# Attention feeding a routed mixture of experts: table stores behind the last mask, four early doubles, first weights in pieces, range count moved to the second unit

## The chip, the core and the metric

The kernel runs on one core of a Trainium2 chip, in 32-bit floats. The metric is the device time of one execution in microseconds (us), as the median of three runs.

The engines are called as in the profile: PE is the matrix engine (TensorE) with its weight loads PEld, DVE is VectorE, ACT is ScalarE, POOL is GpSimd, SP is the sync engine. Each engine works through its own instructions in order. SP starts nearly all plain transfers. POOL starts the indirect ones, which store rows at computed places.

## The reference

```python
def _attn_ref(q, k, v, s):                     # q, k, v: (8, 8, 576, 64)
    scores = scale * np.matmul(q, k.transpose(0, 1, 3, 2))
    causal = np.triu(np.ones((S, S), dtype=bool), k=1)
    cum = np.cumsum(np.maximum(s, 0.0), axis=-1)
    bias = -(cum[:, :, :, None] - cum[:, :, None, :])
    scores = np.where(causal, -1000000000.0, scores + np.minimum(bias, 0.0))
    ...
    return np.matmul(attn, v)                  # attn: softmax of scores

def _moe_ref(x, w_gate, w_local, w1, w2):      # x: (8, 576, 512), 8 experts, F = 1024
    logits = np.einsum('bsd,de->bse', x, w_gate)
    local_gate = 1.0 / (1.0 + np.exp(-np.einsum('bsd,de->bse', x, w_local).squeeze(-1)))
    ...
            fresh_e = int(np.argmax(logits[b, s]))
            if s == 0 or local_gate[b, s] < 0.5:
                e = fresh_e
            else:
                e = prev_e if prev_e >= 0 else fresh_e
            ...
            h = np.maximum(x[b, s] @ w1[e], 0.0)
            out[b, s] = p[e] * (h @ w2[e])     # p: softmax of the logits
```

Each of the 8 x 576 rows that the attention yields goes to one of eight experts: its own best one or, where its local gate is at least one half, that of the row before it. So the rows of one expert are known only once all the rows are counted.

## The kernel before

**Attention.** Each of 8 batches has 4 pairs of heads, 32 pairs in all, and `attention` works in 33 slots. Slot n computes the scores of pair n (`scores`, units u = 0 to 3; matmuls L772 and L781 on PE, exponentials L774 and L782 on ACT) and the values of pair n-1 (`values`, L805 and L808, in two blocks `po0` and `po6`, which DVE scales into `xb` and `lb` at L811, L813 and L815). The exponentials carry no bias of their own: the cumulated `s` goes into the keys and the value rows (`weigh`, L751). The causal triangle is cut by `masked` (L757) on POOL: six `affine_select` in a slot, four for the tiles `e` and, last, two for the small tile `et` of the ragged end. The values of a pair need all of its masked tiles, a slot later. A batch's values (`vTb`, `va`, `vl`) are loaded by SP at the start of slots 4, 8, 12 and so on; the router's logits of a batch are sums over heads of value rows times the gate's weights `wbd` (`value_logits`, L732 and L737).

**Router.** It works in four groups of two batches, 18 columns of 128 rows each. `plan(slot, place, f)` hangs a step into one of four places of a slot: 0 after the first two score units, 1 after `po0`, 2 after the other score units, 3 at the slot's end. After a group's last slot n come `sums`, `product`, `codes`, two turns, `ranks` (three matmuls `pos`, L255 to L257), `rows` (the index `idx` of each row) and `gates`. Then `scatter` stores the group's rows with their index and gate, column by column, into `table` in DRAM, sorted by expert. Each store is a `put` (L294): POOL zeroes one element `gap` and issues one indirect transfer:

```python
self.nc.gpsimd.memset(self.gap, 0.0)
put = self.nc.gpsimd.indirect_dma_start(out=self.halves, in_=src, ...)
self.tc.declare_no_dep(put, group="puts", reason="no two rows of the table are the same")
```

Stores of different columns do not wait for one another. A read of the table waits for the stores before it, and a store waits for the reads before it, since which rows a read takes is known only at run time. The stores of a group were placed four a slot, two at place 1 and two at place 3, from slot n+3 on. `range_ends` (slot 5, one matmul `wep`, L721) gathers cumulated ends for the range count below.

**Experts.** `Experts.run` (L527) takes 24 units in the order of `ORDER`: D is 256 rows of one expert ("double"), S is 128 rows, M is two halves of 64 rows of two experts. `assign` chooses experts and rows of the units from the counts so far. Two doubles are chosen early (`EARLY`), from the counts of the first two groups, in slot 20, so that their weights (`load(0)`, 4 MB in two transfers, slot 23) and rows (`fetch(0)`, `fetch(1)`, slot 24) are on the way while attention still runs. There are four places for weights, and `load` puts one expert's `w1b` and `w2b` into the next one. `fetch(u)` on SP reads the rows of a unit (`xq`, four transfers a piece, L454) and its indices and gates (`gi`, L457) from the table; `turn_x` transposes them on DVE. `layer1` (L469; matmuls L481 for M, L490 for the others), a ReLU on ACT, `layer2` (L505; matmuls L516), the gate's product `y` on DVE (L519) and an indirect store into `out_dram` on POOL (L521) finish a unit. Behind the first layer of unit 0, whose chunks also hold the last group's router steps, stand 8 pads and the 18 stores of the last group, and the choice of all other units. From then on unit u's first layer is followed by `fetch(u + 2)`.

**Range count.** `in_range` (L901) counts on DVE which row sums and ends lie in a safe range (L910 to L917), sums the counts over partitions with a matmul against a tile of ones (`g_ones`, memset on POOL, L919; `g_total`, L921) and writes `out_of`. The program ends by reading that number on the engines; if it is not zero, a general version runs instead. It stood behind everything else.

## Time and profile before

| what | us |
|---|---|
| median of three runs (894.46, 892.03, 897.78) | 894.46 |
| the profiled execution | 900.83 |
| its span on the core | 898.9 |
| PE busy, share of the span | 808.7, 90% |
| POOL busy, share of the span | 214.9, 24% |
| ACT busy, share of the span | 162.0, 18% |
| DVE busy, share of the span | 246.0, 27% |
| matmuls of the experts' first layer, D and S (L490) | 226.1 |
| matmuls of the experts' second layer (L516) | 268.2 |
| issuing 72 table stores on POOL (L297) | 72.2 |

The span runs from the first to the last record of the core; the execution's own time has some 2 us more around it. Busy time is the sum over an engine's instructions. The table says that PE has by far the most work, and that about a tenth of the span it has none. It does not say where. The 72 stores keep POOL for 72.2 us in all, and POOL is idle for three quarters of the span, so as an average POOL is no limit. Whether it is one in the stretch where the stores stand is read from that stretch alone.

### The profile page before, as it was taken

The numbers are of one execution on the slowest core, as the hardware profiler recorded it, in microseconds if no ns is written. First come the engines' busy times: TensorE is split into PE (matmuls) and PEld (weight loads), VectorE is DVE, ScalarE is ACT, GpSimd is POOL, SyncE is SP. The second block draws the span as 40 slices with busy tenths as digits, with TensorE's granted clock in tenths as the row PEclk, the third lists the DMA queues.
The fourth block names the chain that finished last, engine by engine and source line by source line (L and its number), as shares of the span: only waits on it lengthen the run. The fifth ranks groups of instructions, "written<-read, shape, count | busy, mean of one in ns | idle before, by whom it ended". The sixth has DMA issues, their size and how long they took to land.

```text
span 898.9 us, 16140 instructions
## 1 busy us (share of the span) xinstructions
PE 808.7 (90%) x6578; PEld 532.7 (59%) x6578; DVE 246.0 (27%) x663; ACT 162.0 (18%) x292; POOL 214.9 (24%) x488
## 2 busy tenths in 40 slices
PE   6989878987878799549999999999999999999994
PEld 3767656766656576414663763676467556656663
DVE  3524714452344246004004104000400040022001
ACT  2334322322322220100110110110011100111010
POOL 1543257235624635701000000000000000000000
PEclk7999989988978999859999999999999999999998
DMA  8676264544682433979994993976896789587000
GB/s 233 184 215 185 81 188 140 171 133 146 250 254 69 149 131 116 348 283 282 376 290 155 413 272 146 426 245 229 294 399 235 206 335 354 199 247 315 24 22 18
DMA packets 60979, 196.72 MB, mean 219 GB/s; under 512 B 17053, under 2 KB 37021, under 8 KB 52192
## 3 DMA queue, kind: packets, MB, share of 16 engines
q1 hardware_dynamic: 52928, 175.48, 57.0%
q0 software_dynamic: 6880, 20.10, 6.0%
q8 instruction: 54, 0.88, 0.4%
q14 instruction: 29, 0.24, 0.1%
q10 hardware_dynamic: 1088, 0.02, 0.1%
HBM read 174.95 MB, written 21.14 MB: 218 GB/s over the span
## 4 chain that ended last, share of the span: by engine, by line
PE 60%; issue 3%; POOL 1%; DVE 0%; POOLq 0%
PE yp L516 30%; PE hp L490 25%; PE hp L481 5%; POOL table L297 1%; PE po L805 0%; POOL e L758 0%; DVE y L519 0%; DVE g_good L915 0%; DVE g_good L913 0%; DVE g_good L914 0%; DVE g_count L917 0%; PE po L808 0%; POOL et L758 0%; POOL gap L296 0%; DVE g_scaled L910 0%
## 5 line engine op out<-in xcount | busy, mean ns | idle before, releaser
L516 PE MATMUL yp<-w2b,hT 128*128 128x512 f32 (+1 forms) x704 | 268.2, 594 | 0.0
L490 PE MATMUL hp<-xT,w1b 128*128 128x256 f32 (+1 forms) x1152 | 226.1, 357 | 0.0
L490 PEld LDWEIGHTS hp<-xT,w1b 128*128 128x128 f32 x1152 | 198.9, 191 | 32.6 <-issue 10.3
L516 PEld LDWEIGHTS yp<-w2b,hT 128*128 128x128 f32 (+1 forms) x704 | 110.5, 175 | 150.1 <-issue 147.0
L521 POOL DMA_INDIRECT out_dram<-y,gi x38 | 37.2, 980 | 471.1 <-DVE y L519 449.3
L805 PE MATMUL po<-vg,e 128*64 128x75 f32 x3072 | 125.5, 240 | 24.6 <-POOL e L758 23.3
L805 PEld LDWEIGHTS po<-vg,e 128*64 128x64 f32 x3072 | 113.7, 144 | 32.1 <-POOL e L758 25.4
L774 ACT ACTIVATE e<-ps 128x1024 f32<-128x1024 f32 x96 | 95.3, 1023 | 197.4 <-PE ps L772 172.2
L492 ACT ACTIVATE hT<-hp 128x256 f32<-128x256 f32 (+1 forms) x144 | 51.9, 361 | 437.3 <-PE hp L490 437.3
L519 DVE TENSOR_SCALAR y<-yp,gi 128x512 f32<-128x512 f32 x38 | 28.3, 744 | 314.4 <-PE yp L516 314.4
L772 PE MATMUL ps<-qb,kb 64*128 64x512 f32 (+4 forms) x640 | 112.3, 481 | 0.2 <-DMA qb<-in_q_dram 0.2
L758 POOL TENSOR_SCALAR_AFFINE_SELECT e<-e 128x256 f32<-128x256 f32 x128 | 63.8, 521 | 109.5 <-ACT e L774 108.5
L772 PEld LDWEIGHTS ps<-qb,kb 64*128 64x128 f32 x640 | 61.9, 202 | 42.0 <-issue 32.7
L297 POOL DMA_INDIRECT table<-xb,idx x72 | 72.2, 1003 | 44.9 <-issue 19.4
L501 DVE STREAM_TRANSPOSE hT<-hs 32x256 f32<-32x256 f32 x96 | 41.8, 436 | 92.6 <-ACT hs L483 91.3
L481 PE MATMUL hp<-w1b,xT 128*64 128x512 f32 x192 | 45.5, 629 | 23.3 <-issue 23.3
L811 DVE RECIPROCAL recs<-po 128x12 f32<-128x12 f32 x64 | 13.6, 213 | 174.6 <-PE po L805 88.7
L481 PEld LDWEIGHTS hp<-w1b,xT 128*64 128x64 f32 x192 | 14.2, 144 | 50.7 <-issue 50.4
L466 DVE STREAM_TRANSPOSE xT<-xq 128x1024 f32<-128x1024 f32 (+1 forms) x24 | 24.4, 1015 | 35.7 <-DMA xq<-table 35.5
L751 DVE TENSOR_TENSOR vg<-va,wk 128x1184 f32<-128x1184 f32 (+1 forms) x16 | 31.8, 2031 | 0.0
L813 DVE TENSOR_TENSOR xb<-po,recs 128x384 f32<-128x384 f32 x64 | 29.3, 458 | 2.6 <-DVE recs L811 0.5
L758 POOL TENSOR_SCALAR_AFFINE_SELECT et<-et 64x64 f32<-64x64 f32 x64 | 15.4, 240 | 42.5 <-DMA table<-xb,idx 26.9
(212 smaller groups left out, 230.4 us busy)
## 6 DMA issues: line engine op xcount, KB each, us to landing
w1b<-in_w_dram SPq DMA_DIRECT2D x30, 2048.0 KB, 9.7
w2b<-in_w_dram SPq DMA_DIRECT2D x30, 2048.0 KB, 12.4
vTb<-in_vT_dram SPq DMA_DIRECT2D x8, 1280.0 KB, 8.8
kb<-in_k_dram SPq DMA_DIRECT2D x32, 288.0 KB, 3.2
qb<-in_q_dram SPq DMA_DIRECT2D x32, 288.0 KB, 3.8
va<-in_vm_dram SPq DMA_DIRECT2D x8, 1024.0 KB, 10.9
xq<-table SPq DMA_DIRECT2D x56, 130.0 KB, 7.5
xq<-table SPq DMA_DIRECT2D x48, 32.5 KB, 6.4
```

The source lines that it names most:

```text
L297: put = self.nc.gpsimd.indirect_dma_start(out=self.halves, in_=src, element_offset=0, in_offset=None, out_offset=bass.IndirectOffsetOnAxis ...
L481: mm(ps[d, :], lhsT=xT[:, k, d], rhs=self.ws[ls[i]][0][:, k, c * 512 : c * 512 + 512], start=(k == 0), stop=(k == DK - 1))
L490: mm(ps[:, :w], lhsT=self.ws[ls[0]][0][:, k, c * P : c * P + P], rhs=xT[:, k, :w], start=(k == 0), stop=(k == DK - 1))
L492: nc.scalar.activation(self.hT[u][:, c, :w], ps[:, :w], Act.Relu)
L501: self.nc.vector.transpose(hT[32 * a : 32 * a + 32, :, 32 * r : 32 * r + 32], hs[32 * r : 32 * r + 32].rearrange("p (c i) -> p c i", i=P)[ ...
L516: mm(ps[d, :], lhsT=hT[:, k, n * P + i * w : n * P + i * w + w], rhs=self.ws[ls[i]][1][:, k, :], start=(k == 0), stop=(k == FK - 1))
L521: put = nc.gpsimd.indirect_dma_start(out=self.out[:, :], out_offset=bass.IndirectOffsetOnAxis(ap=gi.bitcast(I32)[:, n, 0:1], axis=0), in_= ...
L751: nc.vector.tensor_tensor(vgs[b % 2][g].rearrange("p c h e -> p (c h) e")[:, :, : VW - 1], va.rearrange("p c h e -> p (c h) e")[:, : n * H ...
L758: nc.gpsimd.affine_select(out=ap, in_=ap, compare_op=Alu.is_ge, fill=0.0, base=0, pattern=n, channel_multiplier=-1)
L772: mm(ps[:, h, at : at + z - a], lhsT=kb[d, c * P : c * P + P], rhs=qb[d, a:z], start=True, stop=True)
L774: nc.scalar.activation(e, ps, Act.Exp, scale=scale)
L805: mm(po[d, j - j0, :], lhsT=weights_of(n, c, j, h), rhs=vg[:, c, 2 * hp + h, :], start=(c == 0), stop=(c == last))
```

## The change

What it does, part by part:

- **Stores.** A group's stores stand two a slot instead of four, both at place 3, behind the slot's last mask, from slot n+4 on. The first group has slots 12 to 20, the second 20 to 28, the third 28 to 32 and then eight stores at the start of `Experts.run` (`self.rest`). Slots 20 and 28 have four. `ranks`, `rows` and `gates` move to places 0, 1 and 3 of slot n+3. `idx` has two buffers, since a group's stores now outlast the next group's start.
- **`xb` by batch.** The tile of a group's rows becomes two tiles, one a batch, in four half-size buffers.
- **Four early doubles.** `EARLY` is `(2, 2)`: two chosen in slot 20, two more in slot 28 from the counts of three groups. `ORDER` becomes four D, then four times MDD, then twice MDSS: the same units in another order.
- **First weights in pieces.** `load(0)` goes in four pieces in slots 21 to 24. `fetch(0)` and `fetch(1)` move from slot 24 to slot 29, `turn_x(0)` from slot 28 to 31.
- **Start of the experts.** `run` issues the eight remaining stores, `load(1)`, `fetch(2)`, `turn_x(1)`, `fetch(3)`. Later the first layer of unit u is followed by `turn_x(u + 1)` and `fetch(u + 3)`.
- **Range count.** `in_range` stands behind the first layer of unit 1; its matmul uses a bank of the pool `ps_m`.
- **Small moves.** Router constants in slot 3; the matmul of the range ends in slot 6, a slot behind the work that feeds it; `wbd` is prepared outside the program and loaded in one transfer on SP, instead of a memset on POOL and four transfers on ACT.

The diff, cut to its core:

```diff
-EARLY = 2
+EARLY = (2, 2)
-ORDER = "DD" + "MDD" * 2 + "MDDS" * 4
+ORDER = "DDDD" + "MDD" * 4 + "MDSS" * 2
...
-        idx = st["idx"] = self.s("idx", [P, NC], I32)
+        idx = st["idx"] = self.s("idx", [P, NC], I32, bufs=2)
...
     def scatter(self, g, c):
         st = self.g[g]
-        self.put(st["x"][:, c].rearrange("p g f -> p (g f)"), st["idx"][:, c : c + 1])
+        self.put(st["x"][c // NJ][:, c % NJ].rearrange("p g f -> p (g f)"), st["idx"][:, c : c + 1])
...
-    def assign_early(self):
+    def assign_early(self, i):
+        v = self.nc.vector
         self.counted()
-        self.early, used, _ = self.assign("a", self.shifted("n0", 8), None, EARLY, DOUBLE)
...
+        of, used, _ = self.assign(f"a{i}", n, self.start, EARLY[i], DOUBLE)
+        self.early.append(of)
+        v.tensor_tensor(self.used, self.used, used, op=Alu.add)
...
-        self.p_x = self.x_stack.enter_context(tc.tile_pool(name="p_x", bufs=2, side="right"))
+        self.p_x = self.x_stack.enter_context(tc.tile_pool(name="p_x", bufs=2 * GB, side="right"))
+        self.rest = []
...
-    def load(self, l):
+    def load(self, l, part=None):
...
+        parts = 1 if part is None else 4
+        for t, src in zip(self.ws[l], (self.w1, self.w2)):
+            n = t.shape[1] // parts
+            c = slice((part or 0) * n, (part or 0) * n + n)
+            nc.sync.dma_start(t[:, c].rearrange("p c f -> p (c f)"),
+                              src[bass.ds(self.e, 1), :, c].rearrange("o p c f -> (o p) (c f)"))
...
+        for f in self.rest:
+            f()
         self.load(1)
+        self.fetch(2)
         self.turn_x(1)
+        self.fetch(3)
...
-                    self.fetch(2)
                 else:
-                    self.fetch(u + 2)
-                self.turn_x(u + 1 if u else 99)
+                    self.turn_x(u + 1)
+                    self.fetch(u + 3)
+                if u == 1:
+                    in_range(tc, recs, wend, router.over, out_of, self.ps_m)
...
-        in_range(tc, recs, wend, router.over, out_of)
...
-    nc.gpsimd.memset(wbd, 0.0)
-    for h in range(2):
-        for w, a, z in ((w_gate, 0, E), (w_local, E, E + 1)):
-            nc.scalar.dma_start(wbd[heads[h], :, h * WR + a : h * WR + z],
-                                w.rearrange("(a h d) e -> h d a e", h=2, d=DH)[h])
+    nc.sync.dma_start(wbd, wbd_in)
...
-        plan(n + 2, 2, lambda g=g: router.ranks(g, ps_m))
-        plan(n + 2, 3, lambda g=g: router.rows(g))
-        plan(n + 3, 1, lambda g=g: router.gates(g, of[g][0]))
+        plan(n + 3, 0, lambda g=g: router.ranks(g, ps_m))
+        plan(n + 3, 1, lambda g=g: router.rows(g))
+        plan(n + 3, 3, lambda g=g: router.gates(g, of[g][0]))
         for c in range(NC):
-            plan(n + 3 + c // 4, (1, 3)[c // 2 % 2], lambda g=g, c=c: router.scatter(g, c))
+            if n + 4 + c // 2 <= NPAIR:
+                plan(n + 4 + c // 2, 3, lambda g=g, c=c: router.scatter(g, c))
+            else:
+                experts.rest.append(lambda g=g, c=c: router.scatter(g, c))
+    plan(3, 3, router.constants)
+    plan(5, 1, range_ends)
+    plan(6, 0, range_ends_sum)
     n = 2 * HP * GB
-    plan(2, 3, router.constants)
-    plan(5, 3, range_ends)
-    plan(n + 4, 1, router.assign_early)
-    plan(n + 7, 3, lambda: experts.load(0))
-    plan(n + 8, 1, lambda: (experts.fetch(0), experts.fetch(1)))
-    plan(n + 12, 3, lambda: experts.turn_x(0))
+    plan(n + 4, 1, lambda: router.assign_early(0))
+    for i in range(4):
+        plan(n + 5 + i, 3, lambda i=i: experts.load(0, i))
+    plan(n + 13, 1, lambda: (experts.fetch(0), experts.fetch(1)))
+    plan(n + 12, 1, lambda: router.assign_early(1))
+    plan(n + 15, 3, lambda: experts.turn_x(0))
```

On POOL, one slot with stores, before. The names `e_...` are the tiles of exponentials, `et` that of the ragged end; `x2` is two instructions in a row:

```order
L758 AFFINE_SELECT e_2535<-e_2535 128x2x128
L758 AFFINE_SELECT e_2536<-e_2536 128x2x128
L296 MEMSET gap 1x1
L297 DMA table<-xb,idx 75264x260
L296 MEMSET gap 1x1
L297 DMA table<-xb,idx 75264x260
L758 AFFINE_SELECT e_2537<-e_2537 128x2x128 x2
L758 AFFINE_SELECT et<-et 64x64 x2
L296 MEMSET gap 1x1
L297 DMA table<-xb,idx 75264x260
L296 MEMSET gap 1x1
L297 DMA table<-xb,idx 75264x260
```

The first pair of stores stood ahead of the masks of the second half of the slot, and the second pair behind the last mask. On the same engine after the change, two slots in a row:

```order
L782 AFFINE_SELECT e_2121<-e_2121 128x2x128
L782 AFFINE_SELECT e_2122<-e_2122 128x2x128
L782 AFFINE_SELECT e_2123<-e_2123 128x2x128 x2
L782 AFFINE_SELECT et<-et 64x64 x2
L300 MEMSET gap 1x1
L301 DMA table<-xb,idx 75264x260
L300 MEMSET gap 1x1
L301 DMA table<-xb,idx 75264x260
L782 AFFINE_SELECT e_2286<-e_2286 128x2x128
L782 AFFINE_SELECT e_2287<-e_2287 128x2x128
L782 AFFINE_SELECT e_2288<-e_2288 128x2x128 x2
L782 AFFINE_SELECT et<-et 64x64 x2
```

Only two stores stand in a slot, behind its last mask; ahead of them there is nothing but masks. On SP, the end of attention after the change, from the last keys and queries to the weights of the second unit (TENSOR_LOAD reads the chosen expert and row from memory, ISA rows are address arithmetic):

```order
L651 DMA kb<-in_k_dram 128x576
L652 DMA qb<-in_q_dram 128x576
L437 TENSOR_LOAD a0of
L472 ISA
L472 DMA xq<-table 32x8x130
```

Both early fetches (four `xq` and one `gi` each) now stand behind the last keys and queries, with the second unit's weights behind them; before, they stood between the first unit's weights and the keys of later slots. On POOL, slot 29's two stores come after these reads of the table in the program, and the first of the two waits for all ten of them. On PE, the first units before; `xT` and `hT` are a unit's turned rows and hidden layer, `yp` its output:

```order
L490 MATMUL hp<-xT,w1b 128x256 x8
L516 MATMUL yp<-w2b,hT 128x512 x16
L490 MATMUL hp<-xT,w1b 128x256 x32
L481 MATMUL hp<-w1b,xT 64x512 x16
L516 MATMUL yp<-w2b,hT 128x512 x16
L516 MATMUL yp<-w2b,hT 64x512 x16
L490 MATMUL hp<-xT,w1b 128x256 x32
L516 MATMUL yp<-w2b,hT 128x512 x16
L490 MATMUL hp<-xT,w1b 128x256 x32
L481 MATMUL hp<-w1b,xT 64x512 x16
```

The second unit, a double, and the third, two halves (L481), were taken as a pair here: both first layers, then both second layers. After the change:

```order
L508 MATMUL hp<-xT,w1b 128x256 x8
L534 MATMUL yp<-w2b,hT 128x512 x16
L508 MATMUL hp<-xT,w1b 128x256 x32
L952 MATMUL g_total<-g_count,g_ones 128x1
L534 MATMUL yp<-w2b,hT 128x512 x16
L508 MATMUL hp<-xT,w1b 128x256 x32
L534 MATMUL yp<-w2b,hT 128x512 x16
L508 MATMUL hp<-xT,w1b 128x256 x32
L499 MATMUL hp<-w1b,xT 64x512 x16
L534 MATMUL yp<-w2b,hT 128x512 x16
```

Four doubles come first, and the range count's matmul (L952) stands between the first and the second layer of the second one. The tile of ones that it takes is set on POOL, where after the change these rows stand between the last pads and the outputs of the second unit:

```order
L301 DMA table<-pad,pad_i 75264x260
L300 MEMSET gap 1x1
L301 DMA table<-pad,pad_i 75264x260
L300 MEMSET gap 1x1
L301 DMA table<-pad,pad_i 75264x260
L538 MEMSET gap 1x1
L539 DMA out_dram<-y,gi 4608x512
L538 MEMSET gap 1x1
L539 DMA out_dram<-y,gi 4608x512
L950 MEMSET g_ones 128x128
L538 MEMSET gap 1x1
L539 DMA out_dram<-y,gi 4608x512
```

The memset of ones (L950) has moved from the end of the program to the place behind the first unit's two output stores; ahead of the pads shown stand the last group's 18 stores and the eight of the third group.

More of the change, by code (lines that the diff above doesn't have):

```diff
@@ L66 @@
     w_local: bass.AP,
+    wbd: bass.AP,
     w1: bass.AP,
@@ L85 @@
         with ExitStack() as early:
-            attention(early, tc, q, k, vm, vt, vT, s, w_gate, w_local, ident, recs, wend, router, experts)
+            attention(early, tc, q, k, vm, vt, vT, s, wbd, ident, recs, wend, router, experts)
         experts.run(recs, wend, out_of)
@@ L417, in piece @@
         if kind == "D":
-            of, n = (self.router.early, n) if n < EARLY else (self.router.doubles, n - EARLY)
+            if n < sum(EARLY):
+                of, n = self.router.early[n // EARLY[0]], n % EARLY[0]
+            else:
+                of, n = self.router.doubles, n - sum(EARLY)
         elif kind == "S":
@@ L818, in sums @@
     def sums(g):
-        xb, lb = xs.pop(g)
+        xb, lb = [xs.pop(b) for b in range(g * GB, g * GB + GB)], xs.pop((g, "l"))
         ls = p_ls.tile([P, NC, E + 1], F32, name="ls")
@@ L1437 @@
     v = i["v"]
+    wbd = _np.zeros((2, DH, HP, 2, WR), _np.float32)
+    for h in range(2):
+        for n, w in ((slice(0, E), i["moe_w_gate"]), (slice(E, E + 1), i["moe_w_local"])):
+            wbd[h, :, :, h, n] = w.reshape(HP, 2, DH, -1)[:, h].transpose(1, 0, 2)
     arrays = {
@@ L1446 @@
         "w_local": i["moe_w_local"],
+        "wbd": wbd.reshape(P, HP, 2 * WR),
         "w1": i["moe_w1"].reshape(E, DK, P, F).transpose(0, 2, 1, 3),
```

57 lines of the change are left out of this document (33 added, 24 removed).

## The prediction

> **What bounds the kernel now.** I read the busy time by stage first, then what TensorE (PE) waits for, then the queues behind those waits. The stages are cut at the first score matmul of slot 1, of slot 11, at the first expert matmul (328.46 us, called T below), at both ends of the expert stage's one gap and at the last matmul. Columns: stretch, its length, busy us and instructions of each engine, granted PE clock, DMA share, GB/s.
>
> ```profile
> 18.84:104.62 85.78, 78.39 (x1449) 60.43 (x1442) 40.56 (x114) 31.54 (x42) 33.10 (x99) 0.98 0.60 181
> 104.62:328.46 223.84, 183.92 (x2980) 140.84 (x2977) 86.60 (x269) 65.47 (x86) 111.19 (x239) 0.89 0.50 156
> 328.46:371.21 42.75, 42.73 (x168) 31.42 (x168) 22.75 (x104) 6.08 (x16) 21.26 (x41) 1.00 0.57 208
> 371.21:394.49 23.28, 0.00 (x0) 0.03 (x1) 0.71 (x1) 0.38 (x1) 8.06 (x16) 0.62 0.75 262
> 394.49:404.54 10.05, 10.05 (x33) 3.18 (x33) 0.00 (x0) 0.60 (x1) 0.00 (x0) 0.70 0.93 390
> 404.54:887.24 482.70, 482.68 (x1856) 289.94 (x1856) 87.35 (x152) 52.35 (x139) 36.80 (x70) 1.00 0.71 254
> 887.24:898.90 11.66, 0.35 (x2) 0.30 (x2) 3.57 (x9) 0.00 (x0) 1.20 (x2) 0.70 0.09 31
> ```
>
> PE is full in the experts except for one gap of 23.28 us. In slots 11 to 32, where the table is stored, it is idle for 223.84 - 183.92 = 39.9 us, and its clock stands at 0.89. The price of a slot without stores is that of slot 7, PE full at clock 1.00; the row below it is its value matmuls.
>
> ```profile
> 70.93:77.97 7.04, 7.04 (x128) 5.45 (x125) 5.89 (x9) 3.08 (x4) 3.99 (x5) 1.00 0.27 89
> L805 PE MATMUL po<-vg,e 128*64 128x75 f32 x96 | 3.6, 230 | 0.0
> ```
>
> PE's waits, first in slots 11 to 32, then in slots 1 to 10 (us in total, times, longest):
>
> ```profile
> PE po L805 <- POOL e L758: 22.0, 13, 2.7
> PE po L808 <- POOL et L758: 10.3, 4, 5.9
> PE pos L255 <- DVE incl L246: 5.3, 2, 2.6
> PE pos L255 <- DVE incl L246: 2.6, 1, 2.6
> PE wep L721 <- DVE ends L712: 2.0, 1, 2.0
> ```
>
> So masks on POOL hold PE, and ranks and range ends hold it where they follow their inputs at once. POOL's own rows say why its masks are late: four stores stand in a slot, and the last mask of a slot waits until the stores ahead of it have landed.
>
> ```profile
> 199.09 0.96 POOL L297 DMA_INDIRECT table<-xb,idx  x1 [0.21 <-issue]
> ...
> 206.65 0.24 POOL L758 TENSOR_SCALAR_AFFINE_SELECT et<-et 64x64 f32<-64x64 f32 x1 [5.63 <-DMA table<-xb,idx]
> 206.95 0.09 POOL L296 MEMSET gap<- 1x1 f32 x1
> 207.37 0.98 POOL L297 DMA_INDIRECT table<-xb,idx  x1 [0.33 <-POOL gap L296]
> 208.35 0.09 POOL L296 MEMSET gap<- 1x1 f32 x1
> 208.65 0.96 POOL L297 DMA_INDIRECT table<-xb,idx  x1 [0.21 <-issue]
> ...
> 239.36 0.96 POOL L297 DMA_INDIRECT table<-xb,idx  x1 [0.21 <-issue]
> ...
> 250.49 0.24 POOL L758 TENSOR_SCALAR_AFFINE_SELECT et<-et 64x64 f32<-64x64 f32 x1 [9.20 <-DMA table<-xb,idx]
> table<-xb,idx POOLq DMA_INDIRECT x72, 2.8
> ```
>
> A store with its memset takes 1.28 us (207.37 to 208.65). From its start it lands in 2.8 us (median), in 7.6 beside a batch's value loads (199.09 to 206.65), in 11.1 beside these and the first weights (239.36 to 250.49).
>
> **The change, part by part.** *Slots 11 to 32.* Clean, they would cost 21 x 7.04 = 147.8, a last slot of values alone 3.6 + about 0.3, value logits in four slots (1.5 each by the two rows below), three ranks at 0.7 (339.48 to 340.19 in the chain of waits) and two logit sums at an estimated 0.5: 161 us. They take 223.8, so 62.8 go to waits and to the slow clock that follows them.
>
> ```profile
> L732 PE MATMUL vwp<-vTb,wbd 128*32 128x128 f32 x128 | 4.3, 276 | 0.0
> L737 PE MATMUL vwt<-vTb,wbd 128*32 128x32 f32 x128 | 1.9, 197 | 0.0
> 339.48 0.12 PE pos L255 x2
> 339.60 0.35 PE pos L256 x2
> 339.95 0.24 PE pos L257 x2
> ```
>
> After the change a slot has two stores behind its last mask, and that mask waits for stores of the slot before. POOL's loop is the landing plus 2.0 us (206.65 to 208.65): with 2.8 it is 4.8, under the 7.04 of PE, and it stays under it up to a landing of 5.0. So I take the waits of PE on POOL as gone; what hides the stores is the 2.2 us that POOL then has free in each slot. Slots 20 and 28, with four stores, use that up for one slot. Ranks move a place behind their input, the store's first wait for the gates goes with them.
>
> What stays, or is new: (a) In the slots after value loads the landing of 7.6 exceeds 5.0 by 2.6, four times; half of it reaches PE, since the masks have some 3 us of slack: 4 us (0 to 10). (b) Four half-size buffers: batch 5's first write on DVE waits for batch 1's stores in slot 20; 2 us (0 to 4). (c) The row fetches of units 0 and 1 now stand in slot 29, between stores. They read the table, so slot 29's first store waits for all ten of them to land, and slot 30's masks are queued behind it.
>
> ```profile
> 259.71 1.92 SPq L454 DMA_DIRECT2D xq<-table  x4
> ...
> 265.81 0.40 SPq L457 DMA_DIRECT2D gi<-table  x1
> xq<-table SPq DMA_DIRECT2D x56, 130.0 KB, 7.5
> xq<-table SPq DMA_DIRECT2D x16, 65.0 KB, 20.5
> ```
>
> Counted from the start of slot 29: slot 28's four stores end at 5.4 and land at 7, issuing two fetches takes 6.5 (259.71 to 266.21), and the reads land 2 to 7.5 later (4 taken, little else is moving): 17.5. Without them the store would start at 7.4. Slot 30's first mask then ends at 20.5, where PE wants it at 16.1: 4.4 and a catch-up of 1.6 make 6 us (2 to 11).
>
> *Slots 1 to 10* lose the ranks (2.6 + 0.7) and the wait for the range ends (2.0): 85.78 becomes 80.5. The first weights of the gate come in one transfer on SP instead of four on ACT; PE then still waits for the next keys behind the same value loads, so I put that at 0 (-1 to +3). First expert matmul: 18.84 + 80.5 + 161 + 12 = 272.3, 56.2 earlier.
>
> *The gap.* Its old cause, unit 2 waiting for the last group's rows, goes: units 2 and 3 are early doubles. But the range count's matmul now stands behind unit 1's first layer, and it needs the ones, whose memset stands on POOL behind 8 remaining stores, the last group's 18, 8 pads and unit 0's two output stores.
>
> ```profile
> 357.38 13.83 PE hp L490 x64
> 371.21 23.28 issue
> 343.97 1.01 POOL L297 DMA_INDIRECT table<-xb,idx  x1 [17.59 <-DVE n_i L322]
> ...
> 379.80 0.99 POOL L521 DMA_INDIRECT out_dram<-y,gi  x1 [0.25 <-issue]
> ```
>
> Before, that run of 28 starts at T + 15.5 and ends at T + 52.3. Now its first store also waits for the fetches of units 2 and 3, which wait for the 8 remaining stores: twelve stores of 1.28 from T - 3 end at T + 12.4 and land at T + 15, the fetches issue until T + 21.5 and land 4 later: T + 25.5, 10 us later than before. So the ones are there at T + 62.6, PE is there at T + 42.75 (the third stage's length): a new gap of 19.9 us (9.8 if the fetches cost nothing, 36 if they land after 20.5), with the same slow 10 us at clock 0.70 behind it. Against 23.28 that is a gain of 3.4; the matmul itself costs 0.35. I take off 1 us for weights near the end, where a fetch three units ahead makes SP wait for output stores (0 to 6). The same matmuls run otherwise: units and sizes are unchanged. Net 2.0.
>
> *The end.* 3.6 us of range count leave the chain behind the last matmul. But the last output store is issued at 888.3 too, and SP still waits for it after everything else:
>
> ```profile
> SPq L1455 <- DMA out_dram<-y,gi: 1.5, 1, 1.5
> ```
>
> That transfer then decides the end, so I take 0 (0 to 2).
>
> Sum: 56.2 + 2.0 + 0 = 58.2 us. The profiled execution took 900.83 us (span 898.9), 0.7% over the median of 894.46: 842.6 on its scale, 836 for the median.
>
> The Trainium skill, page "DMA: Bandwidth & Descriptors", section "SWDGE vs HWDGE vs iDMA", says that a DMA engine serves software and hardware queues in turn; by that a store's delay depends on a load being in flight and not on its size, and cutting the first weights in pieces only repeats the delay. The trace half agrees: 7.6 us beside value loads, 11.1 with the weights added, so size does count. By the rule the time is that of rival three.
>
> **Rivals.** *One: the fetches delay nothing* (their landing falls into POOL's other waits). The new gap is 9.8, (c) is 2: 836 - 10 - 4 = 822 to 826. For it: reads that nothing disturbs can land fast. Against: the wait is in the program, and 6.5 us of issue alone remain.
>
> *Two: the fetches land late.* With 20.5 us, the median of 16 fetches behind weights, the gap is 36 and the time 852. For it: unit 1's second weights and unit 2's stand in the same queue. Against: the first are issued at T, the second behind the fetches.
>
> *Three: the pieces repeat the delay.* Each of the four slots with a piece in flight has the 11.1 us landing once seen: 4 x (11.1 - 5.0) = 24, time 860. Against: 1 MB a slot is a quarter of what stood ahead of those stores.
>
> *Four, the other side: the landing wait takes the place of the one removed.* Every one of 21 slots pays landing - 5.0. At 7.8 us in all of them the whole 58 are gone (894), at 8.6 it is 911. For it: 7.6 and 11.1 were seen. Against: the median of 72 is 2.8, and only four slots of 21 have value loads.
>
> **How the numbers follow.** Forecast 836 (829 to 845): 0.54. One: 0.15. Two: 0.12. Three: 0.08. Four: 0.04. The rest, 0.07, is spread outside. 820 to 858 takes in the forecast, one and two. One per cent, about 9 us, is what a measurement here can tell from no change: every case but four is faster by more. Faster 0.95, same 0.02, slower 0.03.
>
> **What would show it.** Right: slots 12 to 28 near 7.04 us, no mask waiting for a store of its own slot, a wait of some 10 us on POOL ahead of slot 29's first store, the first expert matmul near 272, a PE gap of about 20 us in front of the range count's matmul, released by the memset of ones, and an end that still waits for the last output store. Wrong: masks still releasing value matmuls in most slots, no gap ahead of that matmul, or a gap in front of a pair's first layer late in the experts.

## The result, and the profile after

| | median, us | range, us | ratio to before (95% interval) |
|---|---|---|---|
| before, 4 runs | 896.12 | 892.03 to 899.03 | |
| after, 4 runs | 854.95 | 847.43 to 859.67 | 0.9536 (0.9449 to 0.9623) |

The change makes the kernel about 41 us faster. The predicted time was 836, so the median lies 19 us above it, inside the range of 820 to 858. The profiled execution took 851.99 us, its span is 850.3.

The busy time by stage, cut as in the prediction: slots 1 to 10, slots 11 to 32, the first expert unit, the one gap, the slow stretch behind it, the rest, the end. Columns as there: stretch, length, busy us and instructions of PE, PEld, DVE, ACT and POOL, granted clock, DMA share, GB/s.

```profile
18.81:99.42 80.61, 78.16 (x1437) 60.49 (x1437) 35.52 (x107) 31.42 (x42) 30.38 (x98) 0.96 0.62 187
99.42:278.75 179.33, 167.09 (x2985) 128.27 (x2983) 91.31 (x299) 65.15 (x86) 99.06 (x221) 0.99 0.61 189
278.75:325.25 46.50, 38.60 (x130) 25.78 (x128) 23.95 (x107) 3.17 (x9) 27.20 (x54) 0.93 0.69 233
325.25:343.35 18.10, 0.00 (x0) 0.00 (x0) 2.38 (x6) 0.38 (x1) 13.67 (x26) 0.60 0.75 294
343.35:355.23 11.88, 11.88 (x43) 10.01 (x44) 0.00 (x0) 2.27 (x7) 0.25 (x2) 0.75 1.02 427
355.23:843.20 487.97, 487.96 (x1888) 291.33 (x1888) 87.13 (x154) 53.25 (x141) 36.82 (x70) 1.00 0.67 250
843.20:850.30 7.10, 0.00 (x0) 0.00 (x0) 0.75 (x1) 0.00 (x0) 0.98 (x1) 0.80 0.11 43
```

Of the two rows of attention, the first became 5.2 us shorter and the second 44.5: in slots 11 to 32 PE's idle time fell from 39.9 to 12.2 us, its clock rose from 0.89 to 0.99. The experts (T to the end: 571.6 us, 570.4 before) gained nothing. A gap of 18.1 us stands near where the prediction had put one of 19.9. That looks like a confirmation, but its waits are others than the forecast ones. First what PE waits for, over the whole span (us in total, times, longest), then the same for ACT:

```profile
PE hp L508 <- issue: 18.1, 1, 18.1
PE ps L796 <- DMA qb<-in_q_dram: 5.3, 1, 5.3
PE lp L189 <- issue: 5.0, 1, 5.0
PE po L831 <- POOL e L782: 4.5, 2, 2.7
...
PE po L834 <- POOL e L782: 0.2, 1, 0.2
```

```profile
ACT hT L510 <- remote: 58.5, 3, 36.2
```

Masks on POOL now hold PE for 4.5 + 0.2 = 4.7 us, where it was 32.3. The gap stands in front of a first-layer matmul (L508), not of `g_total`, and nothing that the profile shows releases it ("issue"). ACT, which should take those products, is idle for 36.2 us and is released by something that the profile can't name either ("remote"). The start of the experts in time, PE, then ACT, then POOL of the same kernel (start, duration, engine and line, operation, count, idle time and releaser):

```profile
278.75 3.90 PE L508 MATMUL hp<-xT,w1b 128*128 128x256 f32 x16
...
306.17 13.90 PE L534 MATMUL yp<-w2b,hT 128*128 128x512 f32 x32
319.91 5.34 PE L508 MATMUL hp<-xT,w1b 128*128 128x256 f32 x24
343.35 11.76 PE L508 MATMUL hp<-xT,w1b 128*128 128x256 f32 x40 [18.11 <-issue]
354.95 0.28 PE L952 MATMUL g_total<-g_count,g_ones 128*128 128x1 f32 x2
```

```profile
291.31 0.38 ACT L510 ACTIVATE hT<-hp 128x256 f32<-128x256 f32 x1 [19.80 <-remote]
...
342.92 0.38 ACT L510 ACTIVATE hT<-hp 128x256 f32<-128x256 f32 x1 [36.16 <-remote]
```

```profile
277.13 0.98 POOL L301 DMA_INDIRECT table<-xb,idx  x1 [0.28 <-POOL gap L300]
...
278.42 0.96 POOL L301 DMA_INDIRECT table<-xb,idx  x1 [0.21 <-issue]
...
291.07 0.96 POOL L301 DMA_INDIRECT table<-xb,idx  x1 [0.22 <-issue]
...
306.33 1.01 POOL L301 DMA_INDIRECT table<-xb,idx  x1 [13.95 <-DVE be L341]
...
338.08 0.96 POOL L301 DMA_INDIRECT table<-pad,pad_i  x1 [0.23 <-issue]
...
339.35 1.00 POOL L539 DMA_INDIRECT out_dram<-y,gi  x1 [0.22 <-issue]
...
343.26 0.25 POOL L950 MEMSET g_ones<- 128x128 f32 x1
```

How to read them together: PE has the first product of the second unit ready some two microseconds after 319.91, as its 24 matmuls (three products of eight) run at full pace. ACT applies the first ReLU only at 342.92, and PE stops when its product buffers are full. The same happens to the first unit: its first product is begun at T = 278.75 and its first ReLU comes at 291.31, 12.6 us later, where 2.0 to 2.3 is usual. Both delays lie beside a dense run of stores on POOL, one every 1.27 us: twelve from 277.13 to 292.0, and 28 from 306.33 (the last group's stores, the pads and the first unit's outputs). Both end within a microsecond of the run's end. The second also ends at the memset of ones, so this trace alone can't tell it from the predicted cause.

### The profile page after: what moved, and what is told of

Read it like the earlier page. It is cut to its first block, busy times and chain, and to the rows that moved or that the text cites. A ratio compares the mean times of both kernels' runs of the same rounds, so it can differ in the third digit from the quotient of the medians.

```text
span 850.3 us, 16187 instructions
## 1 busy us (share of the span) xinstructions
PE 794.2 (93%) x6578; PEld 522.3 (61%) x6578; DVE 249.8 (29%) x692; ACT 161.2 (19%) x292; POOL 211.5 (25%) x491
## 4 chain that ended last, share of the span: by engine, by line
PE 82%; DMA 4%; issue 4%; POOL 2%; SPq 2%; another core or an unknown queue 2%; DVE 1%; ACT 1%; POOLq 0%; ACTq 0%; DVEq 0%
PE yp L534 31%; PE hp L508 26%; PE po L831 9%; PE ps L796 8%; PE hp L499 5%; DMA table<-xb,idx 3%; SPq L661 1%; DMA vTb<-in_vT_dram 1%; POOL table L301 1%; ACT e L798 1%; PE po L834 1%; PE pt L805 1%; POOL e L782 1%; PE vwp L756 1%
## 5 line engine op out<-in xcount | busy, mean ns | idle before, releaser
L508 PE MATMUL hp<-xT,w1b 128*128 128x256 f32 (+1 forms) x1152 | 232.9, 363 | 19.1 <-issue 18.1
L508 PEld LDWEIGHTS hp<-xT,w1b 128*128 128x128 f32 x1152 | 202.8, 194 | 54.7 <-issue 28.9
L831 PE MATMUL po<-vg,e 128*64 128x75 f32 x3072 | 118.1, 231 | 6.7 <-POOL e L782 4.5
L831 PEld LDWEIGHTS po<-vg,e 128*64 128x64 f32 x3072 | 107.1, 137 | 13.4 <-POOL e L782 4.8
L796 PE MATMUL ps<-qb,kb 64*128 64x512 f32 (+4 forms) x640 | 105.7, 454 | 5.7 <-DMA qb<-in_q_dram 5.3
L796 PEld LDWEIGHTS ps<-qb,kb 64*128 64x128 f32 x640 | 58.1, 190 | 45.1 <-issue 36.0
L837 DVE RECIPROCAL recs<-po 128x12 f32<-128x12 f32 x64 | 13.5, 211 | 120.3 <-PE po L831 60.9
L499 PE MATMUL hp<-w1b,xT 128*64 128x512 f32 x192 | 42.5, 595 | 0.0
```

The costliest lines, as they stand in the source:

```text
L499: mm(ps[d, :], lhsT=xT[:, k, d], rhs=self.ws[ls[i]][0][:, k, c * 512 : c * 512 + 512], start=(k == 0), stop=(k == DK - 1))
L508: mm(ps[:, :w], lhsT=self.ws[ls[0]][0][:, k, c * P : c * P + P], rhs=xT[:, k, :w], start=(k == 0), stop=(k == DK - 1))
L796: mm(ps[:, h, at : at + z - a], lhsT=kb[d, c * P : c * P + P], rhs=qb[d, a:z], start=True, stop=True)
L831: mm(po[d, j - j0, :], lhsT=weights_of(n, c, j, h), rhs=vg[:, c, 2 * hp + h, :], start=(c == 0), stop=(c == last))
```

## The experiments

The theories. **Ones:** the gap is that of the prediction, the second unit waits for the memset of ones behind POOL's stores. **Run:** a dense run of stores itself holds up what PE hands to ACT and DVE, so two stalls stand there, whatever waits for the ones. The runs were made in four groups, each on a chip of its own with the kernel before beside them (medians 896.25, 895.18, 893.61 and 893.92 us there). In the table "first ReLU" is counted from T, and "unit 1" from the start of DVE's work on the first unit's second output product to the second unit's last ReLU, which takes 13.8 us where nothing holds it up. "Gap" is a PE wait in front of `g_total`. The medians are over all runs of a kernel, the other numbers from its one trace. The expectations call Ones theory A and Run theory C; B says that the second unit's results reach ACT late for a cause of their own, D that the row fetches ahead of the run make the stalls, E that the chip or session does.

| kernel | chip | median, us | T | first ReLU | unit 1 | gap |
|---|---|---|---|---|---|---|
| before | | 896.12 | 328.4 | 2.2 | 13.8 | |
| after | | 854.95 | 278.7 | 12.6 | 31.9 | |
| e1, changed kernel | A | 857.13 | 280.3 | 15.7 | 37.7 | |
| e2, ones ready | A | 860.97 | 287.7 | 10.1 | 31.1 | |
| e3, count at the end | A | 863.79 | 290.7 | 8.9 | 31.7 | |
| e4, four a slot | A | 867.39 | 301.4 | 2.3 | 39.1 | |
| e5, spaced | B | 863.12 | 284.8 | 2.0 | 13.8 | 40.9 |
| e6, fetches behind | B | 849.7 | 283.4 | 2.0 | 13.8 | 23.9 |
| e7, no rest | B | 846.88 | 289.3 | 2.0 | 13.8 | 13.0 |
| e8, changed kernel | C | 856.94 | 286.8 | 14.1 | 36.5 | |
| e9, e7 with ones ready | C | 858.53 | 290.7 | 4.6 | 38.0 | |
| e10, e5 with ones ready | C | 842.31 | 280.2 | 5.7 | 13.8 | |
| e11, ones ready | C | 855.6 | 282.1 | 14.3 | 35.8 | |
| e12, e10 and two edits | D | 834.73 | 284.0 | 2.0 | 13.8 | |

**e1: the changed kernel as it is**, as a base for its group.

> The changed kernel as it is, for a second trace and as the measure for the runs beside it. Both theories expect about 855 us and a PE gap of about 18 us in the second unit. What the second trace is to tell: whether the gap again stands inside the second unit's first layer (after 24 of its 64 matmul records, as in the first trace) and ends within 1 us of the memset of ones on POOL.

Measured 857.13 us (855.65 to 866.17), ratio 0.9603 (0.9534 to 0.9672). Both delays are there again. PE again stops after 24 matmuls of the second unit, but it goes on in two parts: at 335.92, which is 11 us ahead of the memset of ones (347.05), and at 349.97, 2.9 us behind it. So the memset does not mark the end of the stall here.

**e2: ones ready.** The range count takes a tile of ones that the router has had since slot 3.

```diff
-    ones = sb.tile([P, P], F32, name="g_ones")
-    nc.gpsimd.memset(ones, 1.0)
-        in_range(tc, recs, wend, router.over, out_of, self.ps_m)
+        in_range(tc, recs, wend, router.over, out_of, self.ps_m, router.ones)
```

> The range count's matmul takes a tile of ones that the router has had since the start, so nothing of it stands on POOL. Theory A (PE's gap is the wait for the ones behind the stores, as the prediction has it): the gap of 18 us goes, with the slow clock behind it (some 10 us at 0.7, 3 us), and the time falls by 15 to 22 us to about 835. Theory B (the gap belongs to the second unit's first layer, whose results reach ScalarE late for a cause of their own): the gap stays and the time stays within 3 us of the changed kernel.

Measured 860.97 us (857.11 to 863.62), ratio 0.9611 (0.9555 to 0.9668): no faster than e1. PE's rows are those of the changed kernel, with the memset gone:

```profile
327.55 5.34 PE L508 MATMUL hp<-xT,w1b 128*128 128x256 f32 x24
352.32 10.88 PE L508 MATMUL hp<-xT,w1b 128*128 128x256 f32 x40 [19.42 <-issue]
```

24 matmuls, and then 19.42 us of nothing. On this chip the ones are not what PE waits for.

**e3: the range count back at the end.**

```diff
-                if u == 1:
-                    in_range(tc, recs, wend, router.over, out_of, self.ps_m)
...
+        in_range(tc, recs, wend, router.over, out_of, self.ps_m)
```

> The range count goes back to the end of the program, all else as changed. Theory A: the gap goes as without the memset (15 to 22 us less), and at the end 0 to 4 us come back, since the count then follows the last output: about 837. Theory B: the gap stays, the end costs 0 to 4 us more: 855 to 859.

Measured 863.79 us (863.65 to 865.04), ratio 0.9643 (0.9598 to 0.9688). With no range count near the second unit, "unit 1" still takes 31.7 us (31.9 and 37.7 in the changed kernel and e1), so the count is not what makes the stall. What its move does bring lies at the end: from the last output product to the end of the span it takes 13.5 us in e3 (849.8 to 863.3) and 7.1 in the changed kernel.

**e4: four stores a slot again**, two at place 1 and two at place 3, still from slot n+4 on. Nothing is left for the experts' start.

```diff
-                plan(n + 4 + c // 2, 3, lambda g=g, c=c: router.scatter(g, c))
+            plan(n + 4 + c // 4, (1, 3)[c // 2 % 2], lambda g=g, c=c: router.scatter(g, c))
```

> Stores go back to four a slot at places 1 and 3, from slot n+4 on, so none is left for the start of the experts; all else as changed. If the stores' place was what made PE wait for masks, the waits of value matmuls for masks come back (about 30 us in the trace before) with the slow clock: the first expert matmul 25 to 40 us later, time 870 to 890. If ranks, pieces and fetches made the gain and the place did not matter, within 8 us of 855.

Measured 867.39 us (867.06 to 869.6), ratio 0.9692 (0.9645 to 0.9739). T comes 21 us later than in e1, and masks are what PE waits for again:

```profile
PE po L834 <- POOL et L782: 6.5, 3, 2.6
PE po L831 <- POOL e L782: 5.9, 3, 4.6
```

The time is only 10.3 us longer, since there is no run of stores at T: the first ReLU comes after 2.3 us, not 15.7. So beside e1 the place of the stores is worth some 21 us of attention, and the eight that it leaves over take about half of that back. The 21 is rough: seven traces with the same attention (the changed kernel, e1, e2, e3, e8, e10, e11) have T anywhere from 278.7 to 290.7, so it is 11 to 23. Both expected ranges are missed: 867.39 lies between "the place is all" and "the place does not matter".

**e5: the stores spaced.** From the experts' start on, six memsets stand before each store instead of one.

```diff
+        for _ in range(self.spaces):
+            self.nc.gpsimd.memset(self.gap, 0.0)
...
+        router.spaces = 6
         for f in self.rest:
             f()
```

> As changed, but from the start of the expert stage on six memsets of the gap stand ahead of each store instead of one, so that stores follow each other at about 2.8 us instead of 1.27. Theory C (an unbroken run of stores holds up the other engines: PE's results reach ScalarE and VectorE many us late): the two stalls shrink, ScalarE's first ReLU of the first unit comes within 4 us of the last values (10.6 and 13 us behind the first expert matmul in the traces so far) and that of the second unit within 6 us of the first unit's last output (19 us so far); the time falls by 10 to 25 us, less what the later stores cost further on (up to 15 us in front of the fifth unit, seen as a new gap). Theory D (the stalls need row fetches just ahead of the run, not its density): both stalls stay, time 855 or more.

**e6: the fetches of units 2 and 3 behind the last group's stores.**

```diff
         self.load(1)
-        self.fetch(2)
         self.turn_x(1)
-        self.fetch(3)
...
+                    self.fetch(2)
+                    self.fetch(3)
```

> As changed, but the row fetches of the third and fourth unit stand behind the last group's stores and pads, as the fetch of the third unit did before the change. Theory D: the stall ahead of the second unit's first ReLU goes (the kernel before has the same run of 28 stores without it), 15 to 20 us less in that place; PE then waits for the third unit's rows, which land at about T + 70 where PE wants them at T + 70 too, so 835 to 845 in all. Theory C: the stall stays as it is (18 to 21 us), 853 to 860.

**e7: no rest.** The third group's stores stand four a slot, at place 3, so that none is left for the experts' start.

```diff
-                plan(n + 4 + c // 2, 3, lambda g=g, c=c: router.scatter(g, c))
-            else:
-                experts.rest.append(lambda g=g, c=c: router.scatter(g, c))
+            plan(n + 4 + c // (4 if g == 2 else 2), 3, lambda g=g, c=c: router.scatter(g, c))
```

> As changed, but the third group's stores stand four a slot at place 3 of slots 28 to 32, so that no store of it is left for the start of the expert stage. Theory C: the first stall (7 to 13 us behind the last values) goes, slots 29 to 32 wait for masks by 2 to 6 us more; the second stall stays; time 846 to 854. Theory D: the first stall stays, since the fetches still stand ahead of these stores: 855 to 862.

Measured: e5 863.12 us (859.6 to 867.48), ratio 0.9647 (0.9592 to 0.9702); e6 849.7 (848.61 to 851.81), ratio 0.9497 (0.9454 to 0.9541); e7 846.88 (844.37 to 850.04), ratio 0.9465 (0.9419 to 0.9511). On this chip there is no stall in any of the three, also not in e7 and e6, whose last run of stores is as dense as that of the changed kernel; e6 has the dense run at T as well. Six memsets make the stores in e5 follow each other at 1.94 us, not at the 2.8 expected. The time of e7 lies in theory C's range, but by luck: the stall that it was to keep is not there, and a gap is there that it did not have. And now the predicted gap is there. PE's wait in e5, in e6, and in e7:

```profile
PE g_total L955 <- POOL gap L540: 40.9, 1, 40.9
```

```profile
PE g_total L952 <- DVE g_count L948: 23.9, 1, 23.9
```

```profile
PE g_total L949 <- POOL gap L538: 13.0, 1, 13.0
```

In e7 and e5 PE waits for POOL, whose queue holds the memset of ones: 13.0 us with the usual stores and none of the eight left over, 40.9 with the spaced ones. In e6 the ones were in time for a gap of about 10 us (PE done at 326.1, memset at 336.06), but the counting itself was late. DVE in e6:

```profile
345.88 1.25 DVE L484 STREAM_TRANSPOSE xT<-xq 128x1024 f32<-128x1024 f32 x1 [32.84 <-DMA xq<-table]
...
349.32 0.45 DVE L948 TENSOR_REDUCE g_count<-g_good 128x1 f32<-128x288 f32 x1
```

The count is queued behind the turning of unit 2's rows, and these rows had been put behind all the stores. So a matmul between two layers of PE waits for the latest of two queues, not for POOL alone.

These three differ from the first group in the chip as well as in the edit, and the changed kernel itself was not run there. So the next group has edits of both kinds on one chip.

**e8: the changed kernel once more.** No edit.

> The changed kernel once more, unchanged, because the three runs before this one had no stall and the five traces before those all had one, whatever their edits. Theory E (the stalls belong to the chip or session a run falls on, not to the edit; the traces with stalls also record only 1 to 6 of the 16 landings of a store that another store follows): where all landings are recorded, the changed kernel has no stall either, and its gap stands in front of the range count's matmul, 18 to 22 us long: 838 to 846. Where landings are missing, it has both stalls and takes about 855. Theory C (the edits removed the stalls): stalls and 855 in both cases.

Measured 856.94 us (853.46 to 859.03), ratio 0.9569 (0.9531 to 0.9606), with both stalls.

**e9: e7 with the ones of the router** (the edits of e7 and e2 together).

> Third group's stores four a slot behind the last mask, none left for the expert stage, and the range count takes the router's ones, so that nothing of it waits for POOL. Without stalls: the 13.0 us in front of the range count's matmul and the slow clock behind them go, 842.5 of span becomes 825 to 830, time 827 to 832. With stalls as in the first traces: one of them left, 840 to 852.

Measured 858.53 us (855.96 to 860.16), ratio 0.9601 (0.9564 to 0.9639). That is a miss for whoever takes e7 for the cure: beside e8 it gains nothing. Its second stall is 38.0 us, where e7 had none on its chip.

**e10: e5 with the ones of the router**, and **e11: e2 once more.** The two differ in the memsets before each store and in nothing else.

> Stores of the expert stage at 2.8 us instead of 1.27 (six memsets), and the ones ready. Theory C: no stall on any chip. Theory E: no stall where landings are all recorded; where they are missing, stalls as ever or shorter. Without stalls the 40.9 us in front of the range count's matmul go, but the last group's stores then end at about T + 100, and PE waits for the fifth unit's rows by 0 to 25 us: 825 to 850.

> As changed with the ones ready, again. Theory A, which fell in the first session: without stalls the gap in front of the range count's matmul goes with its slow clock, 20 to 24 us less than the changed kernel of this call, about 820. With stalls: within 6 us of the changed kernel of this call, as in the first session.

Measured: e10 842.31 us (837.53 to 844.45), ratio 0.9426 (0.9395 to 0.9458); e11 855.6 (854.51 to 858.33), ratio 0.9577 (0.9542 to 0.9611). The ranges don't touch. POOL's stores and ACT's ReLUs in e11:

```profile
318.12 0.96 POOL L301 DMA_INDIRECT table<-xb,idx  x1 [0.22 <-issue]
...
319.38 0.96 POOL L301 DMA_INDIRECT table<-xb,idx  x1 [0.22 <-issue]
```

```profile
308.18 0.38 ACT L510 ACTIVATE hT<-hp 128x256 f32<-128x256 f32 x1 [1.34 <-PE hp L508]
338.13 0.38 ACT L510 ACTIVATE hT<-hp 128x256 f32<-128x256 f32 x1 [29.57 <-POOL gap L300]
348.68 0.94 ACT L510 ACTIVATE hT<-hp 128x256 f32<-128x256 f32 x3 [10.17 <-remote]
```

and in e10:

```profile
313.45 0.96 POOL L303 DMA_INDIRECT table<-xb,idx  x1 [0.16 <-issue]
...
315.39 0.95 POOL L303 DMA_INDIRECT table<-xb,idx  x1 [0.16 <-issue]
```

```profile
301.07 0.38 ACT L512 ACTIVATE hT<-hp 128x256 f32<-128x256 f32 x1 [1.34 <-PE hp L510]
316.59 0.38 ACT L512 ACTIVATE hT<-hp 128x256 f32<-128x256 f32 x1 [15.14 <-PE hp L510]
```

With 1.26 us from store to store (319.38 - 318.12) ACT waits 29.57 us between two units' ReLUs, and then another 10.17; with 1.94 it waits 15.14, which is the second layer of the first unit on PE, and is released by PE's product as it should be. The first ReLU also comes sooner, after 5.7 us instead of 14.3. So on this chip the rate of the stores makes the second stall, and the ones don't; nor do the fetches of theory D, which stand in the same place in both. The spacing has its own price: the first unit's outputs now lie behind slower stores, and PE waits for output buffers.

```profile
PE yp L536 <- DVE y L539: 9.8, 1, 9.8
```

**e12: e10 and two edits.** Five output buffers instead of three against that wait, and the spacing from slot 32 on, so that the stores at T are spaced too.

```diff
-        self.yp = pool("yp", 3)
+        self.yp = pool("yp", 5)
...
+    plan(NPAIR, 0, lambda: setattr(router, "spaces", 6))
```

> The spaced stores with the ones ready, and two edits more: six memsets already from slot 32's stores on, and five output buffers instead of three, since the spaced kernel's PE waited 9.8 us once for an output buffer that a store behind the spaced ones had not yet emptied. Theory C: no stall; the 9.8 us go, with 2 us of slow clock, and 1 to 3 us of the 5.5 between the first expert matmul and the last values: 842.3 becomes 827 to 832. If the stalls come from something else that the spacing only shifted, a new gap of 10 us or more stands in the first three units and the time stays above 838.

Measured 834.73 us (831.03 to 836.7, six runs), ratio 0.9323 (0.929 to 0.9356): faster than both kernels. The first two units run without a pause, the range count's matmul between them:

```profile
298.93 13.90 PE L536 MATMUL yp<-w2b,hT 128*128 128x512 f32 x32
312.66 13.98 PE L510 MATMUL hp<-xT,w1b 128*128 128x256 f32 x64
326.47 0.28 PE L953 MATMUL g_total<-g_count,r_ones 128*128 128x1 f32 x2
```

Experts now take 549.3 us from T to the end, 22 less than in the changed kernel. What is left there is a wait for weights:

```profile
PE hp L501 <- DMA w1b<-in_w_dram: 5.0, 1, 5.0
```

Chip D is one where PE pauses beside stores in attention, as on A and C (next section), so the spacing and not the chip is the likely reason that no stall stands here; that was not tested with an unedited kernel. e12 ran alone on its chip, so how much of its 7.6 us over e10 is due to its two edits and how much to the chip was not measured.

## Why the prediction was right or wrong

*Slots 1 to 10: right.* 80.61 us against 80.5. The price of 0 for the gate's weights held as well: the wait for queries that shows up (5.3 us) lies ahead of 18.81, which is where slot 1 starts in both kernels.

*Slots 11 to 32: the main mechanism right, the sum 6.4 short* (T = 278.75 against 272.3). POOL's masks hold PE for 4.7 us instead of 32.3. Beyond the clean price some 18 us were lost instead of 12, and not one by one as they were put. Slots 22 to 24, 25 and 29 of the changed kernel:

```profile
189.59:211.49 21.90, 21.75 (x379) 16.65 (x373) 9.62 (x23) 9.25 (x12) 14.07 (x30) 1.00 0.81 254
211.49:224.46 12.97, 9.73 (x193) 7.27 (x191) 5.62 (x19) 3.30 (x5) 3.80 (x9) 0.94 0.92 278
...
247.46:256.48 9.02, 8.27 (x129) 5.97 (x125) 2.81 (x15) 3.08 (x4) 6.25 (x15) 1.00 0.23 74
```

The clean price of 161 held: slot 9, with value logits and a logit sum, takes 9.0 (7.04 + 1.5 + 0.5), a slot with ranks 7.9 where 7.7 was taken. Term (a), masks late behind value loads, was 4: in slots 13, 17 and 21 no mask holds PE at all. Slots 13 and 21 are still 2.1 and 2.5 us longer than the 8.5 of the prediction, because PE pauses there, again without a releaser, while POOL issues stores. Slot 13, with stores at 121.99 and 123.27:

```profile
123.27 0.28 PE L761 MATMUL vwt<-vTb,wbd 128*32 128x32 f32 x4 [0.45 <-issue]
124.00 0.28 PE L761 MATMUL vwt<-vTb,wbd 128*32 128x32 f32 x5 [0.45 <-issue]
```

On chip B these two slots take 8.3 to 8.6 us, on A, C and D 10.5 to 13.0. So the 4 us of term (a) were not lost in the way that it says, and that the size is near is luck. The pauses look like a small form of the stall in the experts; that they are the same is not shown. Term (b), the write to a buffer whose stores are still out, was 2 for batch 5; batch 6's write in slot 25 was overlooked, waits 4.64 us on DVE and makes its slot 4.0 us longer than slot 9:

```profile
220.86 0.56 DVE L839 TENSOR_TENSOR xb<-po,recs 128x384 f32<-128x384 f32 x1 [4.64 <-DMA table<-xb,idx]
```

Term (c), the fetches, was 6 and came to 4.3, in slots 31 and 32, where PE waits for masks behind the store that the fetches held. That store starts 17.2 us after slot 29's start, where 17.5 was worked out, and is released by the last of the fetches:

```profile
264.63 0.97 POOL L301 DMA_INDIRECT table<-xb,idx  x1 [7.73 <-DMA gi<-table]
...
267.38 1.79 PE L831 MATMUL po<-vg,e 128*64 128x75 f32 x48 [1.85 <-POOL e L782]
...
275.19 3.35 PE L831 MATMUL po<-vg,e 128*64 128x75 f32 x96 [2.67 <-POOL e L782]
```

Slot 29 itself is 2.0 us longer than 7.0, but all of that is lost ahead of the first fetch (254.84), in pauses like those of slot 13; on chip B it takes 7.0. So the 6.4 us are in the main something that the prediction put at nothing: PE pausing beside stores, 6.6 us in slots 13, 21 and 29. The three terms came to 8.3 instead of 12, and some 3 us more are spread over other slots.

*Rival three: wrong in its size.* The pieces of the first weights are issued at 188.08, 195.96, 203.87 and 220.50. Slots 22 to 24, with the first three in flight, take 21.90 us, 7.3 each, and not 6.1 more than 7.04; PE idles for 0.15 us there. The conclusion that the prediction drew from the rule of the Trainium skill, page "DMA: Bandwidth & Descriptors", section "SWDGE vs HWDGE vs iDMA", that pieces would only repeat the delay, is borne out in part: a store started at 198.70 holds a mask until 205.08, 6.4 us where 2.8 was usual, so a piece does delay it, but not by the 11.1 us of rival three, and the mask was not late enough to hold PE. On chip B such masks did hold PE: in e5 the same three slots take 26.3 us, 5.2 more than clean, where rival three has 18.3 more.

*The gap: right in place and nearly in size, wrong in cause in all three traces of the changed kernel.* That the range count's matmul needs the ones, whose memset stands behind POOL's stores, was forecast to cost 19.9 us. On chip B such a gap is there, 13.0 us in e7 and, for the ones alone, about 10 in e6, where the prediction had 9.8 for the case that fetches cost nothing. In the changed kernel's own trace and on chips A and C its place is taken by a stall that the prediction did not have: with the ones ready (e2, e11) or the count gone (e3) it stands as before. POOL's queue was forecast well: the ones are there at T + 64.5 us, where T + 62.6 was worked out, and the run of 28 starts at T + 27.6 instead of T + 25.5, though the profile names a count on DVE and not the fetches as its release. The step that failed is "the same matmuls run otherwise": it took the 28 stores as a queue that only those behind it wait for, and beside that queue PE reaches the count's matmul at T + 76.2 instead of T + 42.75. The 5 us of PE idle and the slow start of the first unit are its second part. Up to the last matmul the experts became 5.7 us longer; the end gave 4.6 back, so they are 1.1 longer in all, where 2.0 shorter was forecast. That 18.1 stands near 19.9 is luck.

*The end: mis-sized.* 0 (0 to 2) was taken, and 4.6 us were gained: 7.10 us from the last matmul instead of 11.66, and e3 gives them back. "That transfer then decides the end" was wrong: in e3 the last output store is issued at 850.9, the count is done at 854.4, and the end comes 12.4 us behind that store; in the changed kernel the store is issued at 844.3, and the end comes 6.0 behind it. So the count's chain, and what reads its number, had decided the end.

*The scale.* The sum was worked on one execution that stood 6.4 us above its median, and was put down by 6.6 (842.6 to 836). The changed kernel's profiled run stood 3.0 below its median. So of the 19 us, 6.4 are slots 11 to 32, 3.2 the experts with the end, and 9.6 the choice of executions, while single runs of the changed kernel lie up to 12 us apart (847.43 to 859.67).

*What stays open* is why a dense run of stores holds up PE's results on some chips or in some sessions and not in others. Chips B and C differ with nearly the same kernel (e7 and e9), and the changed kernel was not run on B. The kernel before has the same run of 28 and no stall in its trace, but this need not be due to the kernel. The traces divide in the same way by what they record: in the kernel before and on chip B they hold the landings of stores (medians of 2.8 to 3.9 us), in all others the listing has none, as in the changed kernel:

```profile
table<-xb,idx POOLq DMA_INDIRECT x72
```

So whatever differs between these two sorts of traces may make the stall, and the recording itself is not excluded; no run here separates them. e12 is of the second sort and has no stall, so the missing landings do not bring it alone. What inside the chip is held up isn't shown either: where the stalls stand, the profile gives no releaser, a "remote" one or, in e11, a memset on POOL of which the ReLU needs nothing.

## What to carry to other kernels

Read a queue that moves into a stretch where nothing else waits for it not only for what stands behind it, but for its rate: on this kernel, on two of three chips, a run of 28 indirect stores 1.27 us apart cost some 20 us, and five more memsets before each store, which look like waste, made the kernel 13 us faster on the same chip. A gap that ends at the instruction one had expected is no proof of the cause; take the cause away and see if the gap goes, and do it beside the unedited kernel on the same chip. And a small piece of work put between two layers on PE must have all its inputs ahead of it in every queue: the ones on POOL (13.0 us) and the count on DVE (23.9 us) each held it up once.

## What the runs showed of the hardware that was not expected

On chips A and C, stores issued by POOL every 1.27 us delayed the hand-over from PE to ACT and DVE: in the changed kernel, e1, e2, e3, e8 and e11, which all have a dense run of stores at T, ACT's first ReLU comes 8.9 to 15.7 us after T, against 2.2 and 2.3 in the kernel before and e4, which have no run there; at 1.94 us between stores, on the same chip, the second stall is gone (35.8 to 13.8 us). On chip B it did not show at all, also not in e6, which has both dense runs. The stall slows what comes after it too: behind the gap PE works 11.88 us at a granted clock of 0.75. Shorter pauses stand beside two to four stores in slots 13, 21 and 29 of attention, 0.34 to 0.51 us each in the changed kernel's trace; on chip B these slots take some 2 us less.
